# Second MoE of a fused attention and two-MoE kernel: six late weight pieces every four units, remainders on VectorE, 1+u on ScalarE, second GEMM four units behind

## The chip, the core and the metric

The kernel runs on one core of a Trainium2 chip, in one launch. The metric is the device time of that execution in microseconds; lower is better. The version before takes 817.76 us (median of three runs).

## The reference, cut to what matters

Three stages follow each other. An attention with masks (4 x 8 heads, 576 positions) gives 2304 rows of 512. A first mixture of experts sends each row to one of eight experts (512 to 1024 to 512). The third stage, which the code calls the second MoE, is one dense network over all rows, in fp32:

```python
def _moe2_ref(x, w_in, w_out) -> np.ndarray:
    h = x @ w_in
    g = np.maximum(h, 0.0) + np.log1p(np.exp(-np.abs(h)))
    return (g @ w_out).astype(np.float32)
```

Here `x` is [2304, 512], `w_in` [512, 2048] and `w_out` [2048, 512]. The two weights arrive as 64-bit floats, two 32-bit words per number, and have to be converted to fp32 on the chip.

## The kernel before, in words

The order of the instructions on TensorE (PE), VectorE (DVE), ScalarE (ACT) and SyncE (SP) is the order in which the code emits them. Each engine runs its own queue in order. A tile pool with `bufs` buffers makes a new tile wait until the last reader of the tile that had its buffer is done.

**Products in three terms.** Every fp32 operand is split into a high part (an fp32r cast, names ending in h) and a remainder (source minus high part, names ending in l). A product is high x high, high x low and low x high: `mm3` (L894 to L896) for the first GEMM, L1431 to L1433 for the second.

**The second MoE by units.** The 2304 rows are six blocks of 384, and the hidden width 2048 is sixteen slices of 128. A unit is one block with one slice. The list `steps` has 96 units: the first 32 take blocks 0 and 1 in turn, four slices each, then each block takes its sixteen slices. In step i the code emits:

- `gemm1` of unit i (12 matmuls of 384 columns) into one of two psum buffers `pg`, read by abs and relu;
- `gemm2` of unit i - LAG, LAG = 3: for each of three row tiles t, three matmuls of 512 columns into the accumulator q of that tile;
- the softplus in three parts, each of another unit: `softplus_c` of unit i-2 (gh, the cast on ACT; gl, the subtraction on DVE), `softplus_a` of unit i (on ACT u = abs, u = exp(-u), l = relu; on DVE w = 1+u, then u = (w-1)-u), `softplus_b` of unit i-1 (on ACT w = Ln(w); on DVE l = l+w, l = l-u).

The pool `sp` gives two buffers each for u and w and three for l; gh and gl have three.

**The weights.** A piece is 256 of the 2048: even numbers of `w_in`, odd ones of `w_out`. Pieces 0 to 7 (`DIRECT = 8`) are converted during ranks 1 to 5 of the first MoE by `prep_tick`, every fifth of the sixteen steps of a rank: load on SP, abs on ACT, a clamp and three integer steps on DVE (L172, L178, L180, L182), store on SP to a DRAM copy. Later they are loaded as fp32 and split by `piece_hi` (ACT, 128x1024) and `piece_lo` (DVE). Pieces 8 to 15, the late ones, are loaded raw in two halves and converted in the second MoE by `direct(j, step)`: steps 0 and 1 are one half each (abs on ACT into the single buffer `cm`, then the four DVE steps as an iterator in the list `side`), step 2 casts both halves on ACT (wh), step 3 subtracts both halves on POOL (wl). `aside()` takes one instruction from `side` between two softplus instructions of DVE. Piece k of the late ones has its steps at units `D_AT + D_STEP*k + D_OFF[step]`, that is 2 + 3k + (0, 1, 3, 4): one piece every three units. The table `N_HL` gives the units at which prepared pieces are split, counted from the start of rank 7 (16 is unit 0).

**The end.** `END` lists the order of the last second GEMMs. When a tile's accumulator is finished, it is copied (ACT or DVE in turn) and POOL scatters it to the output.

Of the kernel before, what the change touches and what calls it, by code (L numbers as in the profile page):

```python
# [11 lines left out]
F32 = mybir.dt.float32  # L12
# [3 lines left out]
AF = mybir.ActivationFunctionType  # L16
ALU = mybir.AluOpType
# [4 lines left out]
P = 128  # L22
# [5 lines left out]
WARM = 28  # L28
NE_AT = ((6, 14), (7, 0), (7, 1), (7, 2))
X2_AT, X2_HL = (0, 3), ((6, 7, 8, 9), (12, 13, 14, 15))  # L30
N_HL = (8, 10, 12, 14, 16, 18, 20, 22)

D_AT, D_STEP, D_OFF = 2, 3, (0, 1, 3, 4)
XG = 6
IDX_AT, GATHER_AT = 8, 12
TR_AT = (5, 7, 8, 9)
# [6 lines left out]
def attn_moe_softplus_kernel(ctx: ExitStack, tc: tile.TileContext, q, k, v, w_gate, w_ogate, w1, w2, w_in, w_out, out, dbg=None):  # L43
    nc = tc.nc
    B, H, S, D = q.shape
    NT, DM = out.shape
    NE = w_gate.shape[1]
# [5 lines left out]
    NTL = B * NW  # L53
    NC = DM // P
# [5 lines left out]
    const = ctx.enter_context(tc.tile_pool(name="const", bufs=1))  # L60
# [8 lines left out]
    identb = const.tile([P, P], BF16, name="identb")  # L69
    upper = const.tile([P, P], BF16, name="upper")  # L70
    ones = const.tile([P, P], BF16, name="ones")
    wg = const.tile([P, NC, 32], F32, name="wg")
    rev = const.tile([P, NE], F32, name="rev")
    eidx = const.tile([P, NE], F32, name="eidx")
    ebase = const.tile([P, NE], BF16, name="ebase")
    pair = const.tile([P, NTL, 2], I32, name="pair")
    lg = const.tile([P, NTL, 2 * NE], F32, name="lg")
    cumb = const.tile([P, len(GROUPS) + 1, NE], BF16, name="cumb")
    tabi = const.tile([1, 40], I32, name="tabi")
    perm_sb = const.tile([P, NT // P, 2], I32, name="perm_sb")  # L80
# [68 lines left out]
    PC = 512  # L149


    DIRECT = 8
    N_IN, N_OUT = DIRECT // 4, DIRECT // 4 * (PC // P)
    PREP = [(0, r_, c_) for r_ in range(DM // P) for c_ in range(N_IN)] + [(1, r_, 0) for r_ in range(N_OUT)]
    NPREP = len(PREP)
    prep_in, prep_t, prep_n = {}, {}, [0, 0, 0]
# [56 lines left out]

    actx = ExitStack()
    per_p = [None, actx.enter_context(tc.tile_pool(name="per1", bufs=1))]
    mask_w = per_p[1].tile([P, 2, 64], BF16, name="mask_w")
    mask_0 = per_p[1].tile([P, 2, 64], BF16, name="mask_0")
    xt_p = actx.enter_context(tc.tile_pool(name="xt", bufs=2))
# [507 lines left out]
    NF = F2 // P  # L726
# [4 lines left out]
    def sub(e, lo, src, hi):  # L731
        e.tensor_tensor(lo, src, hi.bitcast(F32), ALU.subtract)  # L732
# [12 lines left out]
    pieces = {}  # L745

    def load_piece(r, j, e=None):
        if r == NE and j >= DIRECT:

            pieces[r, j] = []  # L750
            for h in range(2):
                if j % 2 == 0:
                    src = w_in.bitcast(I32)[256 * h : 256 * h + 256, 256 * j : 256 * j + 512].rearrange("(c p) f -> p c f", p=P)
                else:
                    src = w_out.bitcast(I32)[128 * (j - 1 + h) : 128 * (j - 1 + h) + 128].unsqueeze(1)
                t = K["wr"].tile([P, 1024], F32, tag="wr", name=f"wr{r}_{j}{h}").bitcast(I32)
                nc.sync.dma_start(t.rearrange("p (c f) -> p c f", c=src.shape[1]), src)
                pieces[r, j].append(t)
            return
        if r == NE:  # L760
            g = j // 2
            if j % 2 == 0:
                src = w_in32[:, 256 * g : 256 * g + 256].rearrange("(c p) f -> p c f", p=P)
            else:
                src = w_out32[256 * g : 256 * g + 256].rearrange("(c p) d -> p c d", p=P)
        elif j < 4:
            src = w1[ds(e, 1), :, 256 * j : 256 * j + 256].rearrange("o (c p) f -> p (o c) f", p=P)
        else:
            src = w2[ds(e, 1), 256 * (j - 4) : 256 * (j - 3)].rearrange("o (c p) d -> p (o c) d", p=P)
        if r == "v" or r == NE and j < 4:  # L770
            raw_ = K["wa"].tile([P, 1024], F32R, tag="wa", name=f"wr{r}_{j}").bitcast(F32)
        else:
            raw_ = K["wr"].tile([P, 1024], F32, tag="wr", name=f"wr{r}_{j}")
        nc.sync.dma_start(raw_.rearrange("p (c f) -> p c f", c=src.shape[1]), src)
        pieces[r, j] = [raw_]
# [13 lines left out]
    side = []  # L789
# [6 lines left out]
    def direct(j, step):  # L796

        d = pieces[NE, j]
        w_ = [t.bitcast(F32).rearrange("p (n c) -> p n c", c=2)[:, :, 1] for t in d[:2]]
        hs = [slice(512 * h, 512 * h + 512) for h in range(2)]  # L800
        if step < 2:
            m = K["cm"].tile([P, 512], I32, tag="cm", name=f"cm{j}_{step}")
            conv_abs(d[step], m)

            def ops():
                conv_clamp(m)
                yield 1
                for _ in conv_move(d[step], m):
                    yield 1

            side.append(ops())
        elif step == 2:
            p_, kw = (K["w2"], lambda t: dict(tag=t)) if j < 12 else (K["wb"], lambda t: {})
            d += [p_.tile([P, 1024], F32R, name=f"{t}{NE}_{j}", **kw(t)) for t in ("wh", "wl")]
            for h in range(2):
                nc.scalar.copy(d[2][:, hs[h]], w_[h])
        else:
            for h in range(2):
                sub(nc.gpsimd, d[3][:, hs[h]], w_[h], d[2][:, hs[h]])
                load_next()  # L820

    def piece_lo(r, j, eng=None):
        d = pieces[r, j]
# [209 lines left out]
    def tab_load(eng, i, m):  # L1033
        return eng.value_load(tabi[0:1, i : i + 1], min_val=0, max_val=m)
# [4 lines left out]
    def load_next():  # L1039

        nload[1] += 1
        while nload[1] and nload[0] < len(order_):
            r, j = order_[nload[0]]
            two = r == NE and j >= DIRECT
            if two and nload[1] < 2:
                break
            if r not in er and r != NE:
                if not K.get("ranked"):
                    break
                er[r] = tab_load(nc.sync, r, NE - 1)  # L1050
            load_piece(r, j, er.get(r))
            nload[0] += 1
            nload[1] -= 1 + two
# [93 lines left out]
    for i in range(n + 2):  # L1147
# [13 lines left out]
        if i < n:  # L1161
            b, w = tiles[i]
# [51 lines left out]
    while late:  # L1214
# [3 lines left out]
        g = next(g for g, (t0, t1) in enumerate(GROUPS) if t0 <= i < t1)  # L1218
# [88 lines left out]
        sub(nc.vector, x2[b][1][:, cs, :BT], x2[b, h], x2[b][0][:, cs, :BT])  # L1307


    for j, u in enumerate(N_HL):  # L1310
        last_rank.setdefault(u, []).append((hi_, NE, j))
        last_rank.setdefault(u + 1, []).append((lo_, NE, j))
    for b, at_ in enumerate(X2_HL):
# [2 lines left out]
    for r in range(NE):  # L1316
# [8 lines left out]
        for u in range(16):  # L1325
# [27 lines left out]
            if r < NE - 1 or u < 8:  # L1353
                k_ = (r, 4 + u // 2) if u < 8 else (r + 1, (u - 8) // 2)
# [19 lines left out]
    cctx = mctx  # L1374
    K["wb"] = cctx.enter_context(tc.tile_pool(name="wb", bufs=1))
    K["cm"] = cctx.enter_context(tc.tile_pool(name="cm", bufs=1))
    sp_p = cctx.enter_context(tc.tile_pool(name="sp", bufs=2))
    g_p = cctx.enter_context(tc.tile_pool(name="g", bufs=3))
    o_p = cctx.enter_context(tc.tile_pool(name="o", bufs=3))
    ps_g = cctx.enter_context(tc.tile_pool(name="ps_g", bufs=2, space=PSUM))  # L1380
    ps_q = cctx.enter_context(tc.tile_pool(name="ps_q", bufs=2, space=PSUM))
# [13 lines left out]
    def softplus_a(b, f):  # L1395
        u, w_, l = [sp_p.tile([P, BT], F32, tag=t, name=f"{t}{b}_{f}", bufs=3 if t == "l" else None) for t in "uwl"]
        sp[b, f] = (u, w_, l)
        ps = gT[b, f]
        nc.scalar.activation(u, ps, AF.Abs)  # L1399
        nc.scalar.activation(u, u, AF.Exp, scale=-1.0)  # L1400
        nc.scalar.activation(l, ps, AF.Relu)
        nc.vector.tensor_scalar(w_, u, 1.0, None, ALU.add)  # L1402
        aside()
        nc.vector.scalar_tensor_tensor(u, w_, 1.0, u, ALU.subtract, ALU.subtract)  # L1404

# [44 lines left out]

    steps = [(b, 4 * c + f) for c in range(NF // 4) for b in range(2) for f in range(4)]
    steps += [(b, f) for b in range(2, NB) for f in range(NF)]
    LAG = 3
    END = {0: [(NF - 3, (0, 1)), (NF - 2, (0, 1)), (NF - 3, (2,))], 2: [(NF - 1, (0, 1)), (NF - 2, (2,)), (NF - 1, (2,))]}
    pre, post = {}, {}

    def x2_at(b, load, *split):
# [5 lines left out]
    for b in range(2, NB):  # L1463
        s0 = NF * (b - 1)
        x2_at(b, *((s0 + 8, s0 + 12, s0 + 13, s0 + 13, s0 + 14) if b == 2 else (s0 + 4, s0 + 8, s0 + 9, s0 + 10, s0 + 11)))
    for j in range(DIRECT, NF):
        for s in range(4):
            post.setdefault(D_AT + D_STEP * (j - DIRECT) + D_OFF[s], []).append((direct, j, s))
    for i in range(len(steps) + LAG):
        if i < len(steps):  # L1470
            b, f = steps[i]
            for fn, *a in last_rank.get(i + 16, []) + pre.get(i, []):
                fn(*a)
            gemm1(b, f)
        if LAG <= i < len(steps):
            gemm2(*steps[i - LAG])

        for f, ts in END.get(i - len(steps), ()):
            gemm2(NB - 1, f, ts)
        if i < len(steps) - 2:  # L1480
            order_sp = [(2, softplus_c), (0, softplus_a), (1, softplus_b)]
        else:

            order_sp = {
                -2: [(2, softplus_c), (1, softplus_b), (0, softplus_a)],
                -1: [(2, softplus_c), (1, softplus_b), (0, softplus_a), (1, softplus_c)],
                0: [(1, softplus_b), (1, softplus_c)],
            }.get(i - len(steps), [])
        for k_, fn in order_sp:
            if 0 <= i - k_ < len(steps):  # L1490
                fn(*steps[i - k_])
        while side:
            aside()
        for fn, *a in post.get(i, ()):
            fn(*a)
# [28 lines left out]
```

## Time and profile before

| what | value |
|---|---|
| median of three runs (lowest to highest) | 817.76 us (816.33 to 820.75) |
| the profiled execution | 819.59 us |
| its span, first to last instruction | 818.0 us |
| PE busy | 773.8 us (95%) |
| DVE busy | 566.6 us (69%) |
| ACT busy | 471.8 us (58%) |
| POOL busy | 144.6 us (18%) |
| mean granted TensorE clock | 0.986 |

The attention and routing take about the first 150 us, the first MoE goes to about 396 us, and the second MoE fills the rest. A share over the span mixes these stages, so the stretch of the change is read by itself: its windows, its waits, and each engine's timeline.

### The profile page before, as it was taken

The numbers are of one execution on the slowest core, as the hardware profiler recorded it, in microseconds if no ns is written. First come the engines' busy times: TensorE is split into PE (matmuls) and PEld (weight loads), VectorE is DVE, ScalarE is ACT, GpSimd is POOL, SyncE is SP. The second block draws the span as 40 slices with busy tenths as digits, with TensorE's granted clock in tenths as the row PEclk, the third lists the DMA queues.
The fourth block names the chain that finished last, engine by engine and source line by source line (L and its number), as shares of the span: only waits on it lengthen the run. The fifth ranks groups of instructions, "written<-read, shape, count | busy, mean of one in ns | idle before, by whom it ended". The sixth has DMA issues, their size and how long they took to land.

```text
span 818.0 us, 14909 instructions
## 1 busy us (share of the span) xinstructions
PE 773.8 (95%) x5542; PEld 694.5 (85%) x5543; DVE 566.6 (69%) x1112; ACT 471.8 (58%) x909; POOL 144.6 (18%) x170
## 2 busy tenths in 40 slices
PE   6898886999999999999989999999999999999994
PEld 5666664898999999999978887899999999999993
DVE  5767885663667877756799999866656666766662
ACT  4675642344556666566766666656656655655561
POOL 9824343121002012100011222120001001001001
PEclk9999998799999999999999999999999999999998
DMA  9997665255788898669432312220001001001000
GB/s 209 264 243 186 144 159 154 59 193 182 233 275 277 304 299 279 213 216 320 135 103 78 104 53 83 70 85 1 20 0 40 1 1 39 1 0 40 1 1 38
DMA packets 85879, 104.36 MB, mean 128 GB/s; under 512 B 30428, under 2 KB 61404, under 8 KB 85792
## 3 DMA queue, kind: packets, MB, share of 16 engines
q1 hardware_dynamic: 74496, 84.22, 35.7%
q0 software_dynamic: 5104, 13.40, 4.9%
q10 hardware_dynamic: 6192, 5.56, 2.0%
q8 instruction: 57, 0.93, 0.5%
q14 instruction: 30, 0.25, 0.1%
HBM read 83.98 MB, written 19.32 MB: 126 GB/s over the span
## 4 chain that ended last, share of the span: by engine, by line
PE 59%; DVE 12%; issue 9%; ACT 4%; DMA 2%; POOL 1%; POOLq 0%; ACTq 0%; SPq 0%; DVEq 0%
PE pg L895 5%; PE pg L896 5%; PE pg L894 5%; PE q L1433 5%; PE q L1432 5%; PE q L1431 5%; PE ph L894 3%; PE ph L896 3%; PE py L894 3%; PE ph L895 3%; PE py L895 2%; PE py L896 2%; DVE l L1411 2%; PE py L890 2%; PE py L891 2%
## 5 line engine op out<-in xcount | busy, mean ns | idle before, releaser
L895 PE MATMUL pg<-xlm,wh 128*128 128x384 f32 x384 | 129.7, 338 | 0.0
L896 PE MATMUL pg<-xhm,wl 128*128 128x384 f32 x384 | 129.4, 337 | 0.0
L894 PE MATMUL pg<-xhm,wh 128*128 128x384 f32 x384 | 129.4, 337 | 0.0
L1433 PE MATMUL q<-wh,gl 128*128 128x512 f32 x288 | 114.2, 397 | 3.8 <-DVE gl L732 3.8
L1431 PE MATMUL q<-wh,gh 128*128 128x512 f32 x288 | 114.2, 396 | 1.3 <-ACT gh L1417 0.9
L1432 PE MATMUL q<-wl,gh 128*128 128x512 f32 x288 | 113.3, 393 | 0.0
L732 DVE TENSOR_TENSOR wl<-wr,wh 128x1024 fp32r<-128x1024 f32 x72 | 87.6, 1219 | 33.3 <-ACT wh L787 33.3
L1417 ACT CAST gh<-l 128x384 fp32r<-128x384 f32 x96 | 49.2, 513 | 100.5 <-DVE l L1411 100.5
L732 DVE TENSOR_TENSOR gl<-l,gh 128x384 fp32r<-128x384 f32 x96 | 56.6, 590 | 41.3 <-ACT gh L1417 40.2
L787 ACT CAST wh<-wr 128x1024 fp32r<-128x1024 f32 x72 | 75.0, 1047 | 15.2 <-ACT y L917 6.7
L894 PEld LDWEIGHTS pg<-xhm,wh 128*128 128x128 f32 x384 | 72.2, 188 | 3.9
L895 PEld LDWEIGHTS pg<-xlm,wh 128*128 128x128 f32 x384 | 72.1, 188 | 3.8
L1433 PEld LDWEIGHTS q<-wh,gl 128*128 128x128 f32 x288 | 54.1, 188 | 21.9 <-DVE gl L732 10.2
L1402 DVE TENSOR_SCALAR w<-u 128x384 f32<-128x384 f32 x96 | 34.7, 361 | 54.6 <-ACT u L1400 53.9
L896 PEld LDWEIGHTS pg<-xhm,wl 128*128 128x128 f32 x384 | 72.2, 188 | 0.0
L1440 POOL DMA_INDIRECT out_dram<-o,perm_sb x18 | 18.6, 1033 | 271.9 <-DVE o L259 137.4
L1411 DVE TENSOR_TENSOR l<-l,u 128x384 f32<-128x384 f32 x96 | 62.2, 648 | 2.8
L1431 PEld LDWEIGHTS q<-wh,gh 128*128 128x128 f32 x288 | 54.1, 188 | 11.7 <-ACT gh L1417 4.2
L1432 PEld LDWEIGHTS q<-wl,gh 128*128 128x128 f32 x288 | 54.1, 188 | 8.2
L1399 ACT ACTIVATE u<-pg 128x384 f32<-128x384 f32 x96 | 46.9, 489 | 22.9 <-PE pg L896 22.5
L837 POOL DMA_INDIRECT xg<-x_dram,idx x25 | 29.9, 1198 | 167.7 <-ACT wh L787 79.0
L1404 DVE SCALAR_TENSOR_TENSOR u<-w,u 128x384 f32<-128x384 f32 x96 | 53.5, 557 | 2.8
(205 smaller groups left out, 1806.8 us busy)
## 6 DMA issues: line engine op xcount, KB each, us to landing
wr<-in_moe_w_dram SPq DMA_DIRECT2D x64, 512.0 KB, 5.4
raw<-in_q_dram SPq DMA_DIRECT2D x8, 576.0 KB, 7.0
raw<-in_k_dram SPq DMA_DIRECT2D x8, 576.0 KB
x2r<-yT_dram SPq DMA_DIRECT2D x12, 384.0 KB, 4.6
vP<-in_v_dram SPq DMA_DIRECT2D x16, 272.0 KB, 10.8
praw<-in_moe_w_in_dram SPq DMA_DIRECT2D x8, 512.0 KB
praw<-in_moe_w_out_dram SPq DMA_DIRECT2D x8, 512.0 KB, 5.8
wr<-in_moe_w_in_dram SPq DMA_DIRECT2D x8, 512.0 KB
```

What stands on the lines that cost most here:

```text
L732: e.tensor_tensor(lo, src, hi.bitcast(F32), ALU.subtract)
L787: (eng or nc.scalar.copy)(d[1], d[0])
L894: nc.tensor.matmul(ps, wh, xh, start=(first and i == 0), stop=False)
L895: nc.tensor.matmul(ps, wh, xl, start=False, stop=False)
L896: nc.tensor.matmul(ps, wl, xh, start=False, stop=(last and i == k - 1))
L1399: nc.scalar.activation(u, ps, AF.Abs)
L1404: nc.vector.scalar_tensor_tensor(u, w_, 1.0, u, ALU.subtract, ALU.subtract)
L1411: nc.vector.tensor_tensor(l, l, u, ALU.subtract)
L1417: nc.scalar.copy(gT[b, f][0], l)
L1431: nc.tensor.matmul(acc[b, t], gh[:, ts_], wh, start=(f == 0), stop=False)
L1432: nc.tensor.matmul(acc[b, t], gh[:, ts_], wl, start=False, stop=False)
L1433: nc.tensor.matmul(acc[b, t], gl[:, ts_], wh, start=False, stop=(f == NF - 1))
```

## The change

- Pieces 9 and 11 (of `w_out`) are prepared in the first MoE like 0 to 7, by four more preparations, which brings the twenty preparations to the start of rank 6. Six late pieces remain (`LATE`), with steps at 4 + 4k + (0, 1, 3, 3). The split of pieces 9 and 11 is at units 8 and 9, and 14 and 15.
- The remainders of a late piece are subtracted on DVE, through `side`, not on POOL.
- In the first 28 units 1+u is an activation on ACT; after them it stays on DVE.
- The second GEMM is four units behind (LAG = 4), gh and gl have four buffers, and `END` has a new order for the one unit more.
- The parts of the softplus are emitted as a, c, b instead of c, a, b, so abs stands ahead of gh.
- The tiles `wg` and `lg` move to a pool that is closed after the attention.

```diff
@@ -28,9 +28,9 @@
 WARM = 28
 NE_AT = ((6, 14), (7, 0), (7, 1), (7, 2))
 X2_AT, X2_HL = (0, 3), ((6, 7, 8, 9), (12, 13, 14, 15))
-N_HL = (8, 10, 12, 14, 16, 18, 20, 22)
-
-D_AT, D_STEP, D_OFF = 2, 3, (0, 1, 3, 4)
+N_HL = {0: 8, 1: 10, 2: 12, 3: 14, 4: 16, 5: 18, 6: 20, 7: 22, 9: 24, 11: 30}
+
+D_AT, D_STEP, D_OFF = 4, 4, (0, 1, 3, 3)
 XG = 6
 IDX_AT, GATHER_AT = 8, 12
 TR_AT = (5, 7, 8, 9)
@@ -150,7 +148,8 @@
 
 
     DIRECT = 8
-    N_IN, N_OUT = DIRECT // 4, DIRECT // 4 * (PC // P)
+    N_IN, N_OUT = DIRECT // 4, DIRECT // 4 * (PC // P) + 4
+    LATE = [j for j in range(DIRECT, 16) if j not in (9, 11)]
     PREP = [(0, r_, c_) for r_ in range(DM // P) for c_ in range(N_IN)] + [(1, r_, 0) for r_ in range(N_OUT)]
     NPREP = len(PREP)
     prep_in, prep_t, prep_n = {}, {}, [0, 0, 0]
@@ -745,7 +746,7 @@
     pieces = {}
 
     def load_piece(r, j, e=None):
-        if r == NE and j >= DIRECT:
+        if r == NE and j in LATE:
 
             pieces[r, j] = []
             for h in range(2):
@@ -815,9 +816,14 @@
             for h in range(2):
                 nc.scalar.copy(d[2][:, hs[h]], w_[h])
         else:
-            for h in range(2):
-                sub(nc.gpsimd, d[3][:, hs[h]], w_[h], d[2][:, hs[h]])
-                load_next()
+
+            def subs():
+                for h in range(2):
+                    sub(nc.vector, d[3][:, hs[h]], w_[h], d[2][:, hs[h]])
+                    load_next()
+                    yield 1
+
+            side.append(subs())
 
     def piece_lo(r, j, eng=None):
         d = pieces[r, j]
@@ -1041,7 +1047,7 @@
         nload[1] += 1
         while nload[1] and nload[0] < len(order_):
             r, j = order_[nload[0]]
-            two = r == NE and j >= DIRECT
+            two = r == NE and j in LATE
             if two and nload[1] < 2:
                 break
             if r not in er and r != NE:
@@ -1307,7 +1313,7 @@
         sub(nc.vector, x2[b][1][:, cs, :BT], x2[b, h], x2[b][0][:, cs, :BT])
 
 
-    for j, u in enumerate(N_HL):
+    for j, u in N_HL.items():
         last_rank.setdefault(u, []).append((hi_, NE, j))
         last_rank.setdefault(u + 1, []).append((lo_, NE, j))
     for b, at_ in enumerate(X2_HL):
@@ -1374,8 +1380,9 @@
     cctx = mctx
     K["wb"] = cctx.enter_context(tc.tile_pool(name="wb", bufs=1))
     K["cm"] = cctx.enter_context(tc.tile_pool(name="cm", bufs=1))
+    LAG = 4
     sp_p = cctx.enter_context(tc.tile_pool(name="sp", bufs=2))
-    g_p = cctx.enter_context(tc.tile_pool(name="g", bufs=3))
+    g_p = cctx.enter_context(tc.tile_pool(name="g", bufs=LAG))
     o_p = cctx.enter_context(tc.tile_pool(name="o", bufs=3))
     ps_g = cctx.enter_context(tc.tile_pool(name="ps_g", bufs=2, space=PSUM))
     ps_q = cctx.enter_context(tc.tile_pool(name="ps_q", bufs=2, space=PSUM))
@@ -1399,7 +1406,10 @@
         nc.scalar.activation(u, ps, AF.Abs)
         nc.scalar.activation(u, u, AF.Exp, scale=-1.0)
         nc.scalar.activation(l, ps, AF.Relu)
-        nc.vector.tensor_scalar(w_, u, 1.0, None, ALU.add)
+        if steps.index((b, f)) < 28:
+            nc.scalar.activation(w_, u, AF.Copy, bias=1.0)
+        else:
+            nc.vector.tensor_scalar(w_, u, 1.0, None, ALU.add)
         aside()
         nc.vector.scalar_tensor_tensor(u, w_, 1.0, u, ALU.subtract, ALU.subtract)
@@ -1450,8 +1460,7 @@
 
     steps = [(b, 4 * c + f) for c in range(NF // 4) for b in range(2) for f in range(4)]
     steps += [(b, f) for b in range(2, NB) for f in range(NF)]
-    LAG = 3
-    END = {0: [(NF - 3, (0, 1)), (NF - 2, (0, 1)), (NF - 3, (2,))], 2: [(NF - 1, (0, 1)), (NF - 2, (2,)), (NF - 1, (2,))]}
+    END = {0: [(NF - 4, (0, 1, 2)), (NF - 3, (0, 1)), (NF - 2, (0,)), (NF - 3, (2,))], 2: [(NF - 1, (0,)), (NF - 2, (1,)), (NF - 1, (1,)), (NF - 2, (2,)), (NF - 1, (2,))]}
     pre, post = {}, {}
 
     def x2_at(b, load, *split):
@@ -1463,9 +1472,9 @@
     for b in range(2, NB):
         s0 = NF * (b - 1)
         x2_at(b, *((s0 + 8, s0 + 12, s0 + 13, s0 + 13, s0 + 14) if b == 2 else (s0 + 4, s0 + 8, s0 + 9, s0 + 10, s0 + 11)))
-    for j in range(DIRECT, NF):
+    for k_, j in enumerate(LATE):
         for s in range(4):
-            post.setdefault(D_AT + D_STEP * (j - DIRECT) + D_OFF[s], []).append((direct, j, s))
+            post.setdefault(D_AT + D_STEP * k_ + D_OFF[s], []).append((direct, j, s))
     for i in range(len(steps) + LAG):
         if i < len(steps):
             b, f = steps[i]
@@ -1478,7 +1487,7 @@
         for f, ts in END.get(i - len(steps), ()):
             gemm2(NB - 1, f, ts)
         if i < len(steps) - 2:
-            order_sp = [(2, softplus_c), (0, softplus_a), (1, softplus_b)]
+            order_sp = [(0, softplus_a), (2, softplus_c), (1, softplus_b)]
         else:
 
             order_sp = {
```

What the orders show at the three places that matter. The first is ACT in a unit in which the first half of piece 14 has been sent for conversion, before the change (u is abs and exp, l is relu, w is Ln, cm the abs of the weight half; the first number in a name is the slice):

```order
L1417 CAST gh_11_8343<-l_11_8266 128x384
L1399 ACTIVATE u_9_8348<-pg_9_8321 128x384
L1400 ACTIVATE u_9_8348<-u_9_8348 128x384
L1401 ACTIVATE l_9_8350<-pg_9_8321 128x384
L1408 ACTIVATE w_8_8305<-w_8_8305 128x384
L168 ACTIVATE cm_1_8368<-wr_141_8232 128x512
```

and after it:

```order
L1406 ACTIVATE u_9_8344<-pg_9_8322 128x384
L1407 ACTIVATE u_9_8344<-u_9_8344 128x384
L1408 ACTIVATE l_9_8346<-pg_9_8322 128x384
L1410 ACTIVATE w_9_8345<-u_9_8344 128x384
L1427 CAST gh_11_8353<-l_11_8260 128x384
L1418 ACTIVATE w_8_8300<-w_8_8300 128x384
L167 ACTIVATE cm_1_8363<-wr_141_8139 128x512
```

gh went from the first place to behind relu and 1+u (the fourth row), and Ln and the abs of the second half stand behind it.

The second is DVE in the same unit, before:

```order
L732 TENSOR_TENSOR gl_11_8344<-l_11_8266,gh_11_8343 128x384
L172 TENSOR_SCALAR cm_0_8319<-cm_0_8319 128x512
L1402 TENSOR_SCALAR w_9_8349<-u_9_8348 128x384
L178 TENSOR_SCALAR cm_0_8319<-cm_0_8319 128x512
L1404 SCALAR_TENSOR_TENSOR u_9_8348<-w_9_8349,u_9_8348 128x384
L1409 TENSOR_TENSOR l_8_8306<-l_8_8306,w_8_8305 128x384
L180 SCALAR_TENSOR_TENSOR wr_140_8230<-wr_140_8230,cm_0_8319 128x512
L1411 TENSOR_TENSOR l_8_8306<-l_8_8306,u_8_8304 128x384
L182 SCALAR_TENSOR_TENSOR wr_140_8230<-wr_140_8230 128x512
```

and after:

```order
L171 TENSOR_SCALAR cm_0_8320<-cm_0_8320 128x512
L1414 SCALAR_TENSOR_TENSOR u_9_8344<-w_9_8345,u_9_8344 128x384
L733 TENSOR_TENSOR gl_11_8354<-l_11_8260,gh_11_8353 128x384
L177 TENSOR_SCALAR cm_0_8320<-cm_0_8320 128x512
L1419 TENSOR_TENSOR l_8_8301<-l_8_8301,w_8_8300 128x384
L179 SCALAR_TENSOR_TENSOR wr_140_8137<-wr_140_8137,cm_0_8320 128x512
L1421 TENSOR_TENSOR l_8_8301<-l_8_8301,u_8_8299 128x384
L181 SCALAR_TENSOR_TENSOR wr_140_8137<-wr_140_8137 128x512
```

1+u is gone; u now comes ahead of gl, and l-u stays at the end of the unit.

The third is PE at the end of the program: the last matmul of each group of three, before (q_0 to q_2 are the row tiles; the last number before the comma of gh or gl is the slice):

```order
L1433 MATMUL q_0_10762<-wh_15_8581,gl_15_11256 128x512
L1433 MATMUL q_1_10766<-wh_15_8581,gl_15_11256 128x512
L1433 MATMUL q_2_10770<-wh_15_8581,gl_14_11234 128x512
L1433 MATMUL q_2_10770<-wh_15_8581,gl_15_11256 128x512
```

and after:

```order
L1443 MATMUL q_0_10794<-wh_15_8613,gl_15_11257 128x512
L1443 MATMUL q_1_10798<-wh_15_8613,gl_14_11229 128x512
L1443 MATMUL q_1_10798<-wh_15_8613,gl_15_11257 128x512
L1443 MATMUL q_2_10802<-wh_15_8613,gl_14_11229 128x512
L1443 MATMUL q_2_10802<-wh_15_8613,gl_15_11257 128x512
```

Tile 0 is finished one group of three earlier, counted from the end; tile 1 stays two groups from the end.

## Rows read from the trace of the kernel before

**Rows 1.** Windows; columns: from:to, length, busy us and instructions by engine, clock, DMA share, GB/s.

```profile
345.00:360.00 15.00, 15.00 (x124) 15.00 (x123) 8.20 (x11) 9.32 (x16) 0.95 (x1) 1.00 0.76 241
480.00:500.00 20.00, 19.64 (x97) 17.01 (x96) 18.71 (x38) 11.75 (x26) 2.90 (x2) 1.00 0.26 78
540.00:600.00 60.00, 60.00 (x304) 54.51 (x303) 38.61 (x76) 36.26 (x79) 2.88 (x3) 1.00 0.06 20
```

**Rows 2.** Waits of PE from 375 to 818 us: total us, times, longest.

```profile
PE q L1433 <- DVE gl L732: 3.8, 9, 0.8
PE q L1431 <- ACT gh L1417: 0.9, 2, 0.6
```

**Rows 3.** PE's timeline: start, duration, line, tiles, shape.

```profile
395.85 0.34 PE L894 MATMUL pg<-xhm,wh 128*128 128x384 f32 x1
...
404.20 0.40 PE L1431 MATMUL q<-wh,gh 128*128 128x512 f32 x1
...
406.30 0.34 PE L894 MATMUL pg<-xhm,wh 128*128 128x384 f32 x1
...
542.33 0.33 PE L894 MATMUL pg<-xhm,wh 128*128 128x384 f32 x1
```

**Rows 4.** Chain of waits, three units of the second MoE: start, us, what.

```profile
445.88 0.51 ACT gh L1417
...
448.83 1.67 DVE l L1411
...
459.37 0.52 ACT gh L1417
```

**Rows 5.** ACT's timeline; in brackets the idle time before and who ended it.

```profile
398.13 0.49 ACT L1399 ACTIVATE u<-pg 128x384 f32<-128x384 f32 x1
...
412.91 0.49 ACT L1399 ACTIVATE u<-pg 128x384 f32<-128x384 f32 x1
413.43 0.52 ACT L1400 ACTIVATE u<-u 128x384 f32<-128x384 f32 x1
413.86 0.47 ACT L1401 ACTIVATE l<-pg 128x384 f32<-128x384 f32 x1
414.23 0.51 ACT L1408 ACTIVATE w<-w 128x384 f32<-128x384 f32 x1
416.73 0.52 ACT L1417 CAST gh<-l 128x384 fp32r<-128x384 f32 x1 [1.98 <-DVE l L1411]
...
454.59 0.67 ACT L168 ACTIVATE cm<-wr 128x512 f32<-128x512 f32 x1 [1.80 <-DVE wr L180]
...
522.06 0.49 ACT L1399 ACTIVATE u<-pg 128x384 f32<-128x384 f32 x1
```

**Rows 6.** DVE's timeline beside that unit.

```profile
413.05 0.56 DVE L732 TENSOR_TENSOR gl<-l,gh 128x384 fp32r<-128x384 f32 x1 [1.03 <-ACT gh L1417]
...
413.99 0.36 DVE L1402 TENSOR_SCALAR w<-u 128x384 f32<-128x384 f32 x1
414.26 0.42 DVE L178 TENSOR_SCALAR cm<-cm 128x512 int32<-128x512 int32 x1
414.60 0.55 DVE L1404 SCALAR_TENSOR_TENSOR u<-w,u 128x384 f32<-128x384 f32 x1
415.07 0.56 DVE L1409 TENSOR_TENSOR l<-l,w 128x384 f32<-128x384 f32 x1
415.54 0.69 DVE L180 SCALAR_TENSOR_TENSOR wr<-wr,cm 128x512 int32<-128x512 int32 x1
416.14 0.56 DVE L1411 TENSOR_TENSOR l<-l,u 128x384 f32<-128x384 f32 x1
```

**Rows 7.** The page's groups, the cast of a whole weight piece on ACT.

```profile
L787 ACT CAST wh<-wr 128x1024 fp32r<-128x1024 f32 x72 | 75.0, 1047 | 15.2 <-ACT y L917 6.7
```

**Rows 8.** Timeline of the end, ACT and POOL.

```profile
807.43 0.58 ACT L1437 COPY o<-q 128x512 f32<-128x512 f32 x1 [1.45 <-PE q L1433]
...
808.77 0.96 POOL L1440 DMA_INDIRECT out_dram<-o,perm_sb  x1 [0.30 <-issue]
```

More of the change, by code (lines that the diff above doesn't have):

```diff
@@ L71, in attn_moe_softplus_kernel @@
     ones = const.tile([P, P], BF16, name="ones")
-    wg = const.tile([P, NC, 32], F32, name="wg")
     rev = const.tile([P, NE], F32, name="rev")
@@ L76, in attn_moe_softplus_kernel @@
     pair = const.tile([P, NTL, 2], I32, name="pair")
-    lg = const.tile([P, NTL, 2 * NE], F32, name="lg")
     cumb = const.tile([P, len(GROUPS) + 1, NE], BF16, name="cumb")
@@ L215, in attn_moe_softplus_kernel @@
     per_p = [None, actx.enter_context(tc.tile_pool(name="per1", bufs=1))]
+    wg = per_p[1].tile([P, NC, 32], F32, name="wg")
+    lg = per_p[1].tile([P, NTL, 2 * NE], F32, name="lg")
     mask_w = per_p[1].tile([P, 2, 64], BF16, name="mask_w")
```

## Prediction, made before the changed kernel was timed

> **What bounds the kernel now.** I read the windows first. From 540 to 600 us the second MoE runs with PE busy 60.00 of 60.00 us, DVE 38.61, ACT 36.26; from 480 to 500, with late pieces being converted, PE has 19.64 of 20.00 but DVE 18.71 [rows 1]. The granted clock is 1.00 (the 2.4 GHz level) in both, so the clock takes nothing. All of the change outside a few preparations is in this stretch, so I next ask what PE loses there. The waits name 3.8 us for gl and 0.9 us for gh [rows 2], but a restarted matmul is shown longer than a streaming one, so this is too little. PE's timeline gives the whole: four first GEMMs take 404.20 - 395.85 = 8.35 us, 2.09 each; a second GEMM takes 406.30 - 404.20 = 2.10. At 542.33, 34 first and 31 second GEMMs are done; they need 34 x 2.09 + 31 x 2.10 = 136.1 us and took 146.5 [rows 3]. **PE loses 10.4 us here**, and that is all the stage has to give.
>
> Who holds PE? In the chain of waits, gh stands at 445.88 and again three units later at 459.37: 13.49 us for three units, 4.50 each, where PE needs 4.19. Between them the chain goes ACT, DVE, ACT, with a TENSOR_TENSOR of 1.67 us [rows 4] whose like takes 0.56 elsewhere [rows 6]; the subtractions that POOL runs at that time are what the change takes away. DVE looks full, but the chain is a **loop between two engines**, and it has to be followed in one unit:
> - ACT: abs 412.91, exp 413.43, relu 413.86, Ln 414.23, then nothing until the next gh at 416.73, 1.98 us idle, waiting for l [rows 5].
> - DVE: gl 413.05, (clamp), 1+u 413.99, shift 414.26, u 414.60, l+w 415.07, or-step 415.54, l-u 416.14, without a gap [rows 6].
> gh is out 0.55 before gl starts, so this loop, gh to gh, takes 416.73 - 412.50 = 4.23 us. Full DVE time and loop time coincide here; after the change they don't.
>
> **Part by part.**
>
> *1+u on ScalarE.* 28 instructions of 0.36 us leave DVE [rows 6]; ACT gets 28. No row shows this form on ACT; exp (0.52) and Ln (0.51) are the same 128x384 from SBUF to SBUF, and I take 0.51; as bounds the DVE row's 0.36 and the 0.67 of the 128x512 abs (cm) [rows 5]. ACT's load is no problem (11.75 of 20 us in 480 to 500 [rows 1], plus 0.4 per unit). The place is: u on DVE now waits for abs, exp, relu and this, in line. With the spacings of rows 5 the add starts 0.52 + 0.43 + 0.37 = 1.32 after abs, and DVE may start u at 1.32 + 0.51 + 0.03 = 1.86.
>
> The Trainium skill ("ScalarE: Activation LUTs", Rules for kernel authors) says to put adds and the like on VectorE, not ScalarE; here the rows agree on the size (0.36 against 0.51). By that rule this part is a loss. Worked out from the rows: on DVE the add could start when exp ends, u at 1.47 instead of 1.86, 0.39 less in each of the some 17 units that are slower than PE, about 6 us in all.
>
> *abs in front of gh.* abs of unit i+1 writes the u buffer of unit i-1 (two buffers), so it waits for l-u of i-1, which DVE runs in unit i behind u of unit i. That was hidden: gh waited for the same l-u and stood ahead of abs. Now abs opens the loop. Following a unit with a conversion by the spacings of rows 6: u at 1.86, +0.47 gl, +0.47 shift, +0.34 l+w, +0.47 or-step, +0.60 l-u, +0.58 to its end and the next abs: **4.79 us**, against 4.23 now. A unit with the two remainders on DVE: 1.86 + 0.47 + 0.47 + 0.60 (a 128x512 step as the or-step) + 0.58 + 0.58 = 4.56. A unit without either: 3.96. In the first conversion unit of a piece the second cm abs waits for the single cm buffer, as at 454.59 (idle 1.80 [rows 5]); it ends 0.1 later than abs could start: 4.89. Every four units: 4.89 + 4.79 + 3.96 + 4.56 = 18.2, **4.55 each**; now 4.50.
>
> *Remainders on VectorE.* POOL's stretching of DVE's instructions (1.67 for 0.56 and more) goes; DVE pays 2 x 0.60 per piece instead. Included above.
>
> *Six pieces, every four units.* In four units DVE has 4 x 4 x 0.47 = 7.5 us of softplus, 2 x (2 x 0.34 + 2 x 0.60) = 3.8 of conversion and 1.2 of remainders, 12.5 of 16.8, so it is the loop and not DVE's time that bounds. The sum, from the first abs at 398.13 to the one of unit 28 at 522.06 [rows 5], is 123.9 us now. After: the first five steps 2.1 + 3.5 + 3 x 3.96 = 17.5 (PE's pace, then no gh yet, then the plain unit); units 5 to 27 are 6 x 4.89 + 6 x 4.79 + 6 x 3.96 + 5 x 4.56 = 104.6; the casts wh of pieces 7 and 11 stand behind a blocked cm abs in ACT's queue and add 0.95 each (1.05 [rows 7] less what fits), the subtraction of piece 7 about 0.7. Total 124.7: **+0.8 us**.
>
> *Second GEMM four units behind.* gl of a unit has one unit more before PE needs it, so PE's wait moves from gl to the psum of the first GEMM (two banks, read by abs and relu). PE can't run further ahead of the loop for good, so this changes where PE waits, not how long: I take 0 (bounds -1.4 and +1.4: relu ends 0.95 + 0.47 behind abs). The work is only reordered: five first GEMMs now go ahead of the first second GEMM.
>
> *Two pieces prepared earlier.* Four more preparations in ranks 5 and 6 of the first MoE: 4 x 2.2 us on DVE (the four conversion steps), 4 x 0.67 on ACT, and on SP's queue four loads of 512 KB and four stores of 256 KB, which the weight loads queue behind; a store waits for DVE's last step. From 345 to 360 DVE is busy 8.20 of 15 us, the DMA engines 0.76, PE 15.00 [rows 1]: hidden, 0; if the weights came late, up to +2. In the second MoE four raw loads become two; SP has room there.
>
> *wg and lg* only change pools; no instruction is added, so 0.
>
> *End.* The last output copy is ready at 807.43 + 0.58 = 808.01, but POOL issues its scatter at 808.77 [rows 8], 1.26 behind the one before. In the new order tile 0 ends one group of three matmuls (0.68) earlier, so POOL's row of three starts 0.68 earlier: **-0.65 us**.
>
> Sum: +0.8 - 0.65 = +0.15 on the profiled execution's 819.59, which lies 1.8 above the median of the three runs; on the median 817.76 that is **817.9 us**. The add's bounds (0.36 to 0.67 over 28 units, partly covered) give -4 to +4.
>
> **The rivals.**
> 1. *The loop isn't what bounds; DVE's time is.* Then taking 28 adds and POOL's contention off frees PE: it keeps perhaps 1 us of its 10.4, the end gives 0.65, so about 807.7. For it: DVE is at 18.71 of 20, and the relief is real. It also holds in part if the add on ACT is nearer 0.36 (814). Against: ACT's 1.98 us idle behind l shows that the two engines wait for each other, and two u buffers stand in the code.
> 2. *Slower: the add on ScalarE is dearer than Ln.* It stands in series in the loop, so each 0.1 us over 0.51 costs 0.1 in the some 25 looping units, 2.5 us. At 0.67 with the two-engine wait of abs (0.03 to 0.06 more per unit): 4 + 1 = 5, 822.9. It decides from 0.15 us over Ln's row. For it: the 0.67 of cm; against: that one is a third longer.
> 3. *The earlier preparation delays rank 5 or 6*: +2, 819.9. Against: PE is without a gap in 345 to 360 and DVE little over half busy.
>
> **How the numbers follow.** A measurement of this kernel tells about 0.5% (4.1 us) from no change. Forecast (no change to tell, 814 to 822, with rival 3 inside) 0.62; rival 1, whole or half, 0.25, of which a little stays within 0.5%; rival 2, 0.13. So faster 0.24, same 0.63, slower 0.13. The range takes in the greater part of rival 1's and rival 2's sides: 808.5 to 822.
>
> **What would show it.** Right: abs waits on DVE's l in each conversion unit, abs to abs some 4.8 us in two of four units, PE waiting for relu (the psum) at the first GEMM and no longer for gl; DVE's l never above 0.6; DVE below 85% in 440 to 520 though PE waits; about 11 us lost between the first GEMM and unit 34; the last scatter back to back no more. Wrong: PE without waits from 410 to 540 (rival 1), or the add above 0.65 us (rival 2), or a PE wait at 330 to 375 (rival 3).

## The result and the profile after

The changed kernel takes 822.54 us, the one before 817.74 (medians of 22 runs each). The ratio is 1.0051, 95% interval 1.0035 to 1.0067: on 817.74 this is 4.2 us slower (2.9 to 5.5). I had called up to 4.1 us no change to tell; with 22 runs of each it can be told, and the kernel became slower. The profiled execution took 822.12 us, its span is 820.5.

The second MoE first. In the windows of the changed kernel (columns as in [rows 1])

```profile
325.00:390.00 65.00, 64.26 (x523) 63.25 (x522) 49.28 (x74) 41.01 (x69) 3.55 (x2) 1.00 0.88 289
440.00:520.00 80.00, 74.61 (x360) 63.73 (x359) 57.20 (x115) 54.95 (x121) 0.00 (x0) 1.00 0.19 55
480.00:500.00 20.00, 19.03 (x95) 16.47 (x94) 14.50 (x30) 13.59 (x30) 0.00 (x0) 1.00 0.16 47
```

DVE's busy time from 480 to 500 fell from 18.71 to 14.50 us, POOL's to nothing. And PE's fell as well, from 19.64 to 19.03. DVE was unloaded by a fifth, and PE, which sets the pace, did less: this speaks against DVE's load as what PE waits for, and e1 below tests it. The waits of PE from 390 to 585 us name another releaser than [rows 2]:

```profile
PE pg L900 <- ACT l L1408: 7.8, 16, 1.4
PE pg L900 <- issue: 0.5, 1, 0.5
PE pg L902 <- DVE wl L733: 0.3, 1, 0.3
```

gl and gh are gone; the first GEMM waits for relu to free its psum buffer. PE's timeline, answering to [rows 3]:

```profile
395.21 0.34 PE L900 MATMUL pg<-xhm,wh 128*128 128x384 f32 x1
...
408.96 0.34 PE L900 MATMUL pg<-xhm,wh 128*128 128x384 f32 x1
...
422.66 0.45 PE L900 MATMUL pg<-xhm,wh 128*128 128x384 f32 x1 [0.97 <-ACT l L1408]
...
543.25 0.33 PE L900 MATMUL pg<-xhm,wh 128*128 128x384 f32 x1
```

At 543.25, 34 first and 30 second GEMMs are done, 34 x 2.0875 + 30 x 2.10 = 133.98 us of work (2.0875 is 8.35 / 4) in 148.04. PE loses **14.1 us**, where it lost 10.4. I call this number the stage's loss and use it for every run below.

One conversion unit, ACT's timeline (for [rows 5]) and DVE's (for [rows 6]):

```profile
421.19 0.48 ACT L1406 ACTIVATE u<-pg 128x384 f32<-128x384 f32 x1
421.71 0.52 ACT L1407 ACTIVATE u<-u 128x384 f32<-128x384 f32 x1
422.14 0.47 ACT L1408 ACTIVATE l<-pg 128x384 f32<-128x384 f32 x1
422.51 0.51 ACT L1410 ACTIVATE w<-u 128x384 f32<-128x384 f32 x1
422.92 0.50 ACT L1427 CAST gh<-l 128x384 fp32r<-128x384 f32 x1
423.33 0.52 ACT L1418 ACTIVATE w<-w 128x384 f32<-128x384 f32 x1
426.05 0.49 ACT L1406 ACTIVATE u<-pg 128x384 f32<-128x384 f32 x1 [2.20 <-DVE l L1421]
```

```profile
423.06 0.56 DVE L1414 SCALAR_TENSOR_TENSOR u<-w,u 128x384 f32<-128x384 f32 x1 [2.01 <-ACT w L1410]
423.53 0.55 DVE L733 TENSOR_TENSOR gl<-l,gh 128x384 fp32r<-128x384 f32 x1
424.00 0.42 DVE L177 TENSOR_SCALAR cm<-cm 128x512 int32<-128x512 int32 x1
424.34 0.55 DVE L1419 TENSOR_TENSOR l<-l,w 128x384 f32<-128x384 f32 x1
424.81 0.68 DVE L179 SCALAR_TENSOR_TENSOR wr<-wr,cm 128x512 int32<-128x512 int32 x1
425.41 0.55 DVE L1421 TENSOR_TENSOR l<-l,u 128x384 f32<-128x384 f32 x1
```

Each engine sits idle for two microseconds waiting for the other: DVE 2.01 before u (until ACT's 1+u, 0.51 us, is out), ACT 2.20 before the next abs (until l-u is done). abs to abs is 426.05 - 421.19 = 4.86 us; PE needs 4.19. In all, ACT's waits from 400 to 545 us show

```profile
ACT u L1406 <- DVE l L1421: 30.9, 23, 2.2
ACT cm L167 <- DVE wr L179: 10.0, 6, 1.7
```

The end, beside [rows 8]:

```profile
810.42 0.59 ACT L1447 COPY o<-q 128x512 f32<-128x512 f32 x1 [2.13 <-PE q L1443]
...
811.30 0.96 POOL L1450 DMA_INDIRECT out_dram<-o,perm_sb  x1 [0.30 <-ACT o L1447]
```

The last scatter starts 0.29 us after its copy is ready (811.01); before, it was 0.76.

In the first MoE, 325 to 390 us of the kernel before reads

```profile
325.00:390.00 65.00, 64.82 (x531) 64.18 (x530) 42.64 (x61) 40.78 (x68) 2.63 (x2) 1.00 0.77 254
```

so the four preparations put 6.6 us on DVE there. PE gets one wait that the kernel before does not have, for the remainder of the hidden values (hl), which DVE reads out of the psum buffer that PE needs next:

```profile
353.37 0.37 PE L896 MATMUL ph<-xh,wh 128*128 128x280 f32 x1 [0.59 <-DVE hl L914]
```

What it costs is seen from the first matmul of the first MoE, before and after, to the first GEMM of the second (395.85 and 395.21):

```profile
160.53 0.47 PE L894 MATMUL ph<-xh,wh 128*128 128x424 f32 x1 [1.21 <-DVE xl L732]
158.68 0.47 PE L900 MATMUL ph<-xh,wh 128*128 128x424 f32 x1 [1.21 <-DVE xl L733]
```

That is 235.32 us before and 236.53 after: the first MoE takes **1.2 us** longer. The wait of 0.6 us for hl stands in all eight kernels with the four preparations, whose first MoE takes 236.2 to 236.8 us; the four without (before, e6, e7, e9) take 235.3 to 235.9. In the profiled execution of the changed kernel what stands ahead of the first MoE is 1.85 us shorter, which is why the two spans are only 2.5 us apart; in the profiles of e5 to e10 the first MoE starts anywhere from 158.3 to 160.7 us, and whether the moved tiles `wg` and `lg` have a part in it is open.

### The profile page after: what moved, and what is told of

It reads as the page before. It is cut to its first block, busy times and chain, and to the rows that moved or that the text cites. A ratio compares the mean times of both kernels' runs of the same rounds, so it can differ in the third digit from the quotient of the medians.

```text
span 820.5 us, 14994 instructions
## 1 busy us (share of the span) xinstructions
PE 772.5 (94%) x5542; PEld 693.5 (85%) x5543; DVE 546.9 (67%) x1098; ACT 478.9 (58%) x935; POOL 120.1 (15%) x154
## 4 chain that ended last, share of the span: by engine, by line
PE 60%; issue 10%; DVE 9%; ACT 8%; DMA 1%; POOL 1%; POOLq 0%; ACTq 0%; SPq 0%
PE pg L900 5%; PE pg L901 5%; PE pg L902 5%; PE q L1442 5%; PE q L1441 5%; PE q L1443 5%; PE ph L900 3%; PE ph L902 3%; PE ph L901 3%; PE py L900 2%; PE py L902 2%; PE py L901 2%; PE py L896 2%; PE py L897 2%; PE py L898 2%
## 5 line engine op out<-in xcount | busy, mean ns | idle before, releaser
L900 PE MATMUL pg<-xhm,wh 128*128 128x384 f32 x384 | 131.4, 342 | 8.4 <-ACT l L1408 7.8
L1406 ACT ACTIVATE u<-pg 128x384 f32<-128x384 f32 x96 | 47.1, 491 | 126.7 <-PE pg L902 74.6
L733 DVE TENSOR_TENSOR wl<-wr,wh 128x1024 fp32r<-128x1024 f32 (+1 forms) x86 | 98.2, 1144 | 31.1 <-ACT wh L788 30.9
L788 ACT CAST wh<-wr 128x1024 fp32r<-128x1024 f32 x74 | 77.1, 1047 | 15.0 <-ACT y L923 6.1
L1412 DVE TENSOR_SCALAR w<-u 128x384 f32<-128x384 f32 x68 | 24.6, 361 | 89.2 <-ACT u L1407 89.2
L1421 DVE TENSOR_TENSOR l<-l,u 128x384 f32<-128x384 f32 x96 | 53.5, 557 | 2.9
L733 DVE TENSOR_TENSOR gl<-l,gh 128x384 fp32r<-128x384 f32 x96 | 52.9, 551 | 1.2 <-ACT gh L1427 1.2
L1419 DVE TENSOR_TENSOR l<-l,w 128x384 f32<-128x384 f32 x96 | 52.9, 551 | 0.2
```

The lines of the kernel that those rows point to most:

```text
L788: (eng or nc.scalar.copy)(d[1], d[0])
L900: nc.tensor.matmul(ps, wh, xh, start=(first and i == 0), stop=False)
L1419: nc.vector.tensor_tensor(l, l, w_, ALU.add)
L1421: nc.vector.tensor_tensor(l, l, u, ALU.subtract)
```

## The experiments

The theory was the loop: abs, exp, relu, 1+u on ACT, then u, gl, l+w, l-u on DVE, closed through the two buffers of u (abs writes the buffer that l-u of two units before reads last). The rivals: DVE's time bounds (A), the loss lies before the second MoE (B), abs in front helps (C), the fourth unit costs (D). "Ratio" is to the kernel before on the same chip.

| run | ratio (95% interval) | stage's loss, us |
|---|---|---|
| before | 1 | 10.4 |
| changed | 1.0051 (1.0035 to 1.0067) | 14.1 |
| e1: changed, third u buffer | 0.9872 (0.9833 to 0.9911) | 0.3 |
| e2: changed, gh ahead of abs | 0.9901 (0.9865 to 0.9937) | 4.4 |
| e3: changed, 1+u on DVE | 0.9986 (0.9956 to 1.0017) | 8.7 |
| e4: changed, three units behind | 1.0076 (1.0043 to 1.0109) | 15.1 |
| e5: before, six pieces alone | 0.9944 (0.9919 to 0.9969) | 3.7 |
| e6: before, remainders on DVE alone | 0.9971 (0.9937 to 1.0005) | 8.5 |
| e7: before, abs ahead of gh alone | 1.0085 (1.0056 to 1.0114) | 15.2 |
| e8: changed, e2 and e3 together | 0.9886 (0.9857 to 0.9914) | 1.5 |
| e9: before, 1+u on ACT alone | 1.0031 (1.0015 to 1.0048) | 13.4 |
| e10: e8 and the third u buffer | 0.9891 (0.9858 to 0.9923) | 1.5 |

The chip of e1 to e4 ran the kernel before in 829.86 us (median), so there the ratios compare, not the times.

**e1: a third buffer for u.** To make room, gl goes from four buffers to three, which can't be what helps.

```diff
-    u, w_, l = [sp_p.tile(..., bufs=3 if t == "l" else None) for t in "uwl"]
+    u, w_, l = [sp_p.tile(..., bufs=3 if t in "ul" else None) for t in "uwl"]
-    gT[b, f] = [g_p.tile(...) for t in ("gh", "gl")]
+    gT[b, f] = [g_p.tile(..., bufs=3 if t == "gl" else None) for t in ("gh", "gl")]
```

> The changed kernel with a third buffer for u (gl gets three buffers instead of four, to make room). Theory (the loop of abs, exp, relu, 1+u on ScalarE and u, gl, l+w, l-u on VectorE closes through the two u buffers): abs need not wait for l-u any more, TensorE's waits for relu go from 7.8 us to under 1, and the kernel falls from 822.5 by the some 13 us that the stage loses to 809 to 812. Rival A (VectorE's time bounds): the same work is left on VectorE, so no change, 822 to 823. Rival B (the loss lies before the second MoE, in the four earlier preparations or the moved tiles): no change, 822 to 823.

Measured: 0.9872, on 817.74 this is 807.3 us, 15 below the changed kernel (the stage explains 13.8). No instruction was taken away, and the loss fell from 14.1 to 0.3. Its window, ACT's longest waits and PE's only wait:

```profile
440.00:520.00 80.00, 80.00 (x405) 72.68 (x404) 65.67 (x133) 63.06 (x137) 0.00 (x0) 1.00 0.24 71
```

```profile
ACT u L1406 <- PE pg L902: 12.2, 13, 1.9
ACT cm L167 <- DVE wr L179: 11.4, 6, 2.6
```

```profile
PE pg L900 <- ACT l L1408: 0.4, 1, 0.4
```

abs waits for PE now, no longer for l. PE is busy 80.00 of 80 us with DVE doing more per microsecond than in the changed kernel (65.67 against 57.20). Rivals A and B fall.

**e2: gh ahead of abs again.**

```diff
-            order_sp = [(0, softplus_a), (2, softplus_c), (1, softplus_b)]
+            order_sp = [(2, softplus_c), (0, softplus_a), (1, softplus_b)]
```

> The changed kernel with the old order of the softplus parts, gh ahead of abs. Theory: gl then runs while ScalarE is still at abs to 1+u, and 0.47 of gl leaves the loop while 0.42 of gh enters it beside an idle VectorE; followed unit by unit with the durations of before it loses 3 to 4 us in place of 11, so 814 to 816. Rival A (VectorE's time): no change, 822 to 823. Rival C (abs in front helps, since the psum is freed earlier): slower, 824 to 827.

Measured: loss 4.4 (expected 3 to 4), ratio 0.9901, 809.6 on 817.74: lower than expected. The stage and the end explain 6.0 + 0.5 us below before, the first MoE takes 1.1 us more (236.42): 5.4 us in all, 0.9934, which lies just in the interval; for more there is no evidence. Rival C falls: PE's wait on relu goes from 7.8 to 2.2 us.

```profile
PE pg L900 <- ACT l L1408: 2.2, 4, 1.3
```

**e3: 1+u on VectorE.**

```diff
-        if steps.index((b, f)) < 28:
+        if steps.index((b, f)) < 0:
```

> The changed kernel with 1+u on VectorE in all units. Theory: u may start 0.39 us earlier in each unit (1.47 us after abs instead of 1.86), which takes about 5 us off: 817 to 818.5. Rival A (VectorE's time): 28 x 0.36 = 10 us come back on VectorE; slower, 826 to 832. Rival B: no change.

Measured: 0.9986 (816.6 on 817.74, a little lower than expected), loss 8.7: 5.4 us won by giving DVE 10 us more of work. Rival A expected the opposite sign.

```profile
PE pg L900 <- ACT l L1408: 4.1, 11, 1.2
```

**e4: three units behind.** LAG also sets the buffers of gh and gl, which go back to three.

```diff
-    LAG = 4
+    LAG = 3
-    END = {0: [(NF - 4, (0, 1, 2)), ...
+    END = {0: [(NF - 3, (0, 1)), ...
```

> The changed kernel with the second GEMM three units behind, as before, and the old order at the end. Theory: the loop is the same and TensorE waits at gl instead of at the psum; the stage is the same within 1 us and the end loses the 0.6 us of the scatters: 822.5 to 824. Rival D (the fourth unit is what costs, because TensorE's work is put off while it waits): faster, 818 to 820.

Measured: 1.0076 (824.0 on 817.74), loss 15.1, 1.0 more than in the changed kernel. PE waits at the second GEMM again, but for gh and not, as expected, for gl:

```profile
PE q L1441 <- ACT gh L1427: 6.4, 14, 1.7
```

From the 35th first GEMM on, the span holds 9.2 us more than PE's work in the changed kernel and 11.5 here (9.7 before): with abs in front, gh comes late where ACT also copies a finished output (copy at 566.26, abs 566.75, gh 568.08, and PE's second GEMM starts only at 568.63; again at 703.06), and the scatters are back to back. So in this order the fourth unit is worth 2.3 us behind the stage and 1.0 in it by the profiles, and rival D falls; by the times alone e4 and the changed kernel can't be told apart.

**e5: the pieces alone.** On the kernel before:

```diff
-D_AT, D_STEP, D_OFF = 2, 3, (0, 1, 3, 4)
+D_AT, D_STEP, D_OFF = 4, 4, (0, 1, 3, 3)
+    LATE = [j for j in range(DIRECT, 16) if j not in (9, 11)]
...
```

> The kernel before with the pieces alone: 9 and 11 prepared in the first MoE, six late pieces every four units; remainders still on POOL, 1+u on VectorE, old order, second GEMM three units behind. Theory: of every four units one has no conversion and the loop regains there; followed unit by unit, the second MoE loses 4 to 5.5 us in place of 10.4 before the 35th first GEMM, and the first MoE nothing: ratio to before 0.993 to 0.995. Rival B (the earlier preparations delay the first MoE): ratio 1.000 to 1.003, and waits of TensorE in ranks 5 and 6.

Measured: 0.9944, loss 3.7, a little better than expected. In ranks 5 to 7 PE has one wait of 0.6 us for hl, as in the changed kernel, and the first MoE takes 236.22 us in place of 235.32: rival B holds for 0.9 us here, 1.2 in the changed kernel, and no more.

```profile
PE q L1434 <- DVE gl L733: 1.4, 3, 0.9
PE q L1432 <- ACT gh L1418: 0.6, 1, 0.6
```

**e6: the remainders alone.**

```diff
-                sub(nc.gpsimd, d[3][:, hs[h]], w_[h], d[2][:, hs[h]])
+                sub(nc.vector, d[3][:, hs[h]], w_[h], d[2][:, hs[h]])
...
+            side.append(subs())
```

> The kernel before with the remainders alone moved from POOL to VectorE. Theory: two subtractions of 0.6 us enter every third unit, but the 1.67 us of l-u and the 1.00 of gl beside POOL's work go back to 0.56; the stage loses 6 to 7 us in place of 10.4: ratio 0.995 to 0.997. Rival A (VectorE's time is what bounds): 16 x 0.6 = 9.6 us more of work against some 8 x 1.6 of stretching, no gain to tell: 0.999 to 1.003.

Measured: 0.9971 (0.9937 to 1.0005), loss 8.5, expected 6 to 7. The loop gained, but once a remainder, now in line on DVE, came too late for the first GEMM:

```profile
PE q L1438 <- DVE gl L732: 4.0, 8, 1.2
PE pg L901 <- DVE wl L732: 1.6, 1, 1.6
PE q L1436 <- ACT gh L1422: 0.3, 1, 0.3
```

By the time alone it can't be told from no change.

**e7: abs ahead of gh alone.** The line of e2, put the other way round into the kernel before.

> The kernel before with the order alone: abs ahead of gh. Theory: the loop closes through the two u buffers and gl falls into it; the stage loses 15 to 18 us in place of 10.4: ratio 1.005 to 1.010. Rival C (abs in front is of use by itself): ratio below 1.000.

Measured: 1.0085, loss 15.2 (and 1.7 more after it, as in e4).

**e8: e2 and e3 together.**

> The changed kernel with two parts taken back: gh ahead of abs again and 1+u on VectorE in all units; six pieces, remainders on VectorE and the fourth unit stay. Theory: these two parts are all that costs; the stage loses 1 to 2.5 us, ratio to before 0.986 to 0.990, near the one with a third u buffer. Rival: the fourth unit or the remainders on VectorE cost as well, then the loss stays above 4 us, the ratio above 0.992.

Measured: 0.9886, loss 1.5. In the stage the two parts taken back are what costs, all but 1.5 us. Its window has DVE busier than in the changed kernel (70.36 against 57.20) and PE next to full:

```profile
440.00:520.00 80.00, 79.96 (x402) 71.89 (x401) 70.36 (x144) 55.46 (x118) 0.00 (x0) 1.00 0.22 70
```

**e9: 1+u alone on ScalarE**, the lines of the change put into the kernel before.

> The kernel before with 1+u alone on ScalarE in the first 28 units. Theory: u starts later in the loop, which is not made up by the 0.36 us that VectorE is spared; the stage loses 12 to 14 us in place of 10.4: ratio 1.002 to 1.005. Rival A (VectorE's time bounds, so 10 us less of its work must help): ratio 0.990 to 0.997.

Measured: 1.0031, loss 13.4. DVE is spared 10 us and the kernel is slower: rival A once more.

```profile
PE q L1434 <- ACT gh L1420: 3.5, 8, 0.6
PE q L1436 <- DVE gl L732: 3.4, 8, 0.9
```

**e10: all of it**, the edits of e1, e2 and e3.

> The changed kernel with the third u buffer, gh ahead of abs and 1+u on VectorE: the candidate for the fastest. Theory: the stage loses 0 to 1 us, so it is no more than 1.5 us below the kernel with two parts taken back (ratio 0.9886 to before) : 0.985 to 0.989. Rival: the three-buffer u helps elsewhere too, below 0.983.

Measured: 0.9891, loss 1.5, not below 1 as expected: PE has one wait for relu (0.9 us) in e8 and here. e1, e8 and e10 can't be told apart by their intervals; each beats both kernels by some 9 us and more. e1 has the lowest ratio and the smallest loss. Beside the order and the add of before, the third buffer brings nothing more (1.5 in e8 and e10).

## Why the prediction was right or wrong

**What bounds.** Right for the changed kernel: the bound was the loop of two engines, not DVE's time. e1 shows it: one more buffer, no work less, and 13.8 of the 14.1 us are gone. In the kernel before, where DVE stood at 18.71 of 20 us, loop and DVE's time coincide, as I had said, and no run parts them cleanly: e9 shows only that taking 10 us off DVE doesn't help when it goes into the other arm of the loop.

**The time.** 822.54 lies 0.5 us above the upper end of my range; the ratio on the base of the forecast, 817.76, gives 821.9, just below it. Forecast was +0.15 us, measured +4.2. I had drawn that end for a dearer add, which did not come, so it is luck that the range reaches this far.

**The unit after the change.** Right in kind, short in size. Forecast against the trace, abs to abs: conversion units 4.89 and 4.79 against 4.91 and 4.86; plain 3.96 against 4.05; with remainders 4.56 against 4.66. The price taken for 1+u (0.51) is what the row shows. **The term that was too small is the link from l-u to abs**, which I took from gh as 0.03 us: in the row above l-u ends at 425.96 and abs starts at 426.05. From 395 to 585 us the median is 0.09 (27 cases), for gh before it is 0.03 (32 cases). Up to unit 27, 18 of the abs waited for l-u directly: 0.06 x 18 = 1.1 us. I had put this in rival 2 as a side remark instead of in the sum.

**The sum.** I had +0.8 us for the stage; it lost 3.7 more than before. Up to the abs of unit 27 the loop took 122.5 us (before 120.4; my steps gave 120.7): +2.1, of which 1.8 was not in my steps. The link makes 1.1 of it, the rest is a few hundredths per unit in the other spacings. PE's wait at the psum instead of at gl was taken as 0 with a bound of 1.4; worked out by PE's work, the 30th first GEMM of the changed kernel starts 521.46 - 395.21 = 126.25 us after the first one, behind 29 first and 25 second GEMMs; the kernel before had that work done after 123.39 (it restarts at 519.71 with two matmuls, 0.47 us, more): 2.9 more, so 0.8 on top of the loop. Then PE waited twice more, before the 31st and 32nd (at 525.88 and 530.61), after ACT had split the next block's input (casts of 0.83 at 523.67 and 0.82 at 526.55) while the loop had not caught up: another 0.8, which my sum held only in part.

**The other terms.** The preparation was taken as 0, with up to +2: it cost 1.2, so this term failed as well, and a PE wait at 330 to 375, the sign I had named for rival 3, is there at 353.37. The end gave 0.5 (807.00 to 808.77 between the last matmul and the last scatter, then 810.00 to 811.30), forecast 0.65. 3.7 - 0.5 + 1.2 = 4.4 us is what the profiles explain; the ratio says 4.2 (2.9 to 5.5). The other signs came: PE's wait moved from gl to relu, DVE's load fell to 72% in 440 to 520, l never took over 0.6 us; the loss was 14.1 where I had said about 11.

**The rivals.** Rival 1 (DVE's time) fell with e1, e3 and e9. Rival 2 came true by its smaller half: the add was no dearer than Ln, but the two-engine wait of abs was there (1 us by my price, 1.1 measured). That its time, 822.9, is nearer to the measured one than the forecast is luck. Rival 3 came true by 1.2 of its 2 us. The Trainium skill's rule ("ScalarE: Activation LUTs", Rules for kernel authors: adds on VectorE) was right for this kernel; by that rule I had put about 6 us on the part, and e3 gave 5.4.

**What the change holds.** Pieces alone -6.7 us of loss, remainders alone -1.9; abs in front alone +4.8, 1+u alone +3.0. Together the last two cost 12.6 (14.1 against 1.5), more than the 7.8 that they cost alone. Gains and losses of ten microseconds stood against each other, and the 4 us were their difference, not a small effect.

## What to carry to other kernels

Where two engines hand a value to and fro, add up one round of the loop, link by link, before counting busy time. DVE's share did not tell PE's loss here: it was busy 88% of 440 to 520 us with 1.5 us lost in the stage (e8), 72% with 14.1 lost (the changed kernel), and taking 10 us of work off it made the kernel slower (e9). Look for the buffer that closes the loop: in the changed order one more tile of 1.5 KB per partition took the loss from 14.1 to 0.3 us, more than the two helpful moves together (8.6). When an order is changed, ask which instruction now stands first behind the other engine's result, and what only starts after it.

## What the runs showed of the hardware

An instruction on ACT that was released by DVE's l-u started 0.03 us after it where it waited for DVE alone (gh, median of 32 cases before, 36 in e5, 35 in e8), and 0.09 us after it where it also had a wait for PE, long fulfilled (abs, 27 cases in the changed kernel, 18 in e7, 20 in e4). The trace shows what stands between: for the abs at 426.05, line L1406 from 424 to 428 us lists

```profile
L1406 ACTq EVENT_SEMAPHORE  x1: 17/17/17, 426.0 to 426.0; - x1
L1406 ACT ACTIVATE u<-pg x1: 493/493/493, 426.0 to 426.0; 128x384 f32<-128x384 f32 x1
```

The first is an instruction that only waits, for DVE. It starts at 425.99, 0.03 us after l-u, and abs 0.06 after it. 26 of the 27 abs have one in front; the other, at 536.43, waits for DVE alone, has none, and started 0.03 us after l-u:

```profile
L1406 ACT ACTIVATE u<-pg x1: 492/492/492, 536.4 to 536.4; 128x384 f32<-128x384 f32 x1
```

So the 0.06 us go with the second wait; no run takes it away by an edit. The Trainium skill ("Perfetto Trace Analysis", Identifying Dependency Chains) says that an instruction which waits for several engines may get an instruction in front of it that holds the additional wait; the trace agrees, with the 26 cases.
